# One quarter's attention moved into its own PSUM, the last stores merged over two queues, and the last fifth of a planned kernel in a new order

## The chip, the cores and the metric

The kernel runs on one core of one Trainium2 chip. Its time is device microseconds of one execution. Before the change, three timed runs gave 257.56, 256.4 and 254.25 us; the median, 256.4 us, is the time before. One more execution was profiled; it took 252.56 us.

## The reference

The reference mixes two branches over the same input `x` (2048 rows, 512 channels, bf16) with a gate for each row:

```
g = sigmoid((x * gate_w).sum(-1))
a = long convolution of x with K, plus x * Dskip     # K[d, l] from A, B, C (512 x 128 states), 2048 taps, by FFT
q, k, v = x @ wqkv in 32 heads of 16
phi(z) = [softmax(z @ w_phi), softmax(-(z @ w_phi))]
b = (phi(q) (phi(k)^T v) / (phi(q) . sum phi(k))) @ wo
out = g * a + (1 - g) * b
```

The state-space branch `a` needs, for each channel, a kernel `K` of 2048 taps made from 128 complex exponentials, and then a convolution of 2048 rows with it. The attention branch `b` is linear in the rows once `phi(k)^T v` is known.

## The kernel before, in words

**Layout.** The 2048 rows are held as 16 tiles `j` of 128 rows (row = 64 q + 4 j + c, with q on 32 and c on 4 of the partitions' parts). The 512 channels are four quarters `Q` of 128. `xT` holds the input transposed and later, quarter by quarter, the finished output, from which the stores read.

**Making the taps.** The channels go in 16 units `U` of 32. For one unit (function `kgen`) VectorE builds the table `A` by two products (L1109, L1114) and, unless the unit's digit in `FOURS` is 1, adds them (L1119); it builds `R` by two products (L1126, L1130) from `E` and `cs`, which ScalarE makes. TensorE then multiplies them (L181, tile `kps`): 64 matmuls, or 128 where the sum was left out, since TensorE then adds four terms instead of two. There is one buffer for `A`, so the next unit's L1109 waits for this unit's L181.

**The convolution of a quarter** (function `transform`) runs through TensorE, an eviction to SBUF by ScalarE or VectorE, and so on: `kps`, `KD` (eviction), `psA` (L188), `XA` (eviction), `psB` (L194, or L1228 for the last unit), `XK` (eviction), `t` = `XUX` * `XK` on VectorE (L1302; L1305 and L1240 for units 14 and 15), `psz` (L1328, L1256), `Zr` (eviction). `Zr` goes to DRAM and comes back rearranged as `ZT` (L1343, L1362, on SyncE's queue), or for units 14 and 15 through a transpose on VectorE (`ZS`, L1353 and L1271). Last comes `psy` (L1391) and the multiplication by the gate on VectorE (L1402, L1400), which writes `xT`. Quarters 0 to 2 are done 128 channels at a time, quarter 3 as units 12 and 13 together (64 channels), then 14, then 15, the last one split in halves.

**The attention.** For quarters 0 to 2 the sums of attention are added in the same PSUM tile `psy` by L822 and L824 (`attn`, four matmuls and one for each row tile), before L1391 adds the convolution, so that one multiplication by the gate does both. That holds for row tiles 0 to 11. The attention of tiles 12 to 15 (512 rows) is computed late, in a block of its own (`block(3, True)`): for them the plain convolution of quarters 0 to 2 is copied to `Y` by ScalarE (shown as `Ctab`, whose memory it uses), and a tile `bps` of 512 columns adds up attention of all quarters (L948), the skip term of quarter 3 (L950) and `Y` (L951). It is evicted by L149 (quarter 3) and L983 or L985 (quarters 0 to 2, times the gate) and stored by L997.

**Stores.** Each store of a quarter's output (L1413) is four DMAs, one for each `c`, of 32 partitions. Quarters 0 and 1 are stored as a pair (runs of 512 bytes), quarter 2 alone (256 bytes), quarter 3 in two goes of 64 channels (128 bytes), all by SyncE's queue.

**The order.** Nothing is scheduled when the kernel runs: functions add steps to a plan (`Plan.add`, `Plan.dma`), and `run` walks them in the order of one long string, `ORDER`. That order is at once the order on each engine. Three more strings choose, step by step, between ScalarE and VectorE (`SIDES`), between two rings of PSUM buffers (`RINGS`, two buffers each), and the four-term form (`FOURS`). `NEAR` lists the quarters whose attention of tiles 12 to 15 is added in their own PSUM; it is empty before. Each engine works strictly in its order, so a step that waits holds up all that stand behind it.

Of the kernel before, what the change touches and what calls it, by code (L numbers as in the profile page):

```python
# [10 lines left out]
ACT = mybir.ActivationFunctionType  # L11
# [59 lines left out]
class Plan:  # L71
# [14 lines left out]
             "babhbbclchcCb5b6b7bocDbcdYcibpcHcsd-dZcjctbicIbqbdbebfcmd_9Q9R9SeUcnbwcve0eVbjcue19T9U9Vbkcybxe2brcwe3e4bs9Zczcxcoe59-eL"  # L86
             "cqcp9_cAeMeWcEdOcrdSezeAeBa09W9X9Ya1dTcFbtbubvdRdWcGbycJbze6e7e8cKbAcLblbmbna2cMeRcNcPcQcRcOdQeNe9eaeba3eOc_eSedeeefeceP"
             "d7eQd0d1egd8bBbCbDcScTcUdPeTdUdVeXe-d2d9eYcVcWcXbEbFbGe_dfdgeZdXdhbKdad3dbdncYcZc-bLfAdof0d4d5d6fBbMdcdddef1difVf2djdpfD"
             "bHbIbJf4dqf3ehf5bNfCdrfEf6eibOfWf7ejfeekfGeCeDeEfffFbPfHdkdldmdBbQdsdtduf8eIeJeKdvdwdxf9f_fgfIfafJfhfKdCfXfifYdydzdAfbfc"
             "fdg0fjfkflfZf-eFeGeHfLdEfMdFfNdGdDg1g2dHg3elg4dIdJdKemfmfnfog5g6fpfqfrfOepfPg7eqengadLdMdNeofQg8gbg9fRgderfsbRbSbTgcesbU"  # L90
             "bVbWgffSfTftgeggghgieteuevewexeyfufvfwfxfyfzfUgjgkglgmgngogpgqgr")
    SIDES = ("100001110111000000000101000101010111101001011100000000000100101010000001110001001010100000000000000010000000000000000000"
             "0000000000000001001100000000000000001101100000")
    RINGS = ("101000001110010101100000000000000000000000100000000000000001011100100000001111101101110000100001001110011110100111101101"
             "1010011")
# [716 lines left out]
def plan_queries(P, nc, g, psum, r):  # L812
# [14 lines left out]
    def block(b, late, yn=()):  # L827
        Q, L = Bag(), "L" if late else ""
# [88 lines left out]
        pb, po, ot, out = None, None, [], []  # L917
# [24 lines left out]

        nn = 3 - len(P.NEAR)

# [22 lines left out]
        on = []  # L967
        for ip in range(2 if late else 0):
            j = 4 * b + 2 * ip
# [24 lines left out]
        if late:  # L994
            def st(h):
                for c in (2 * h, 2 * h + 1):
                    (nc.scalar if P.cur.at == "ACT" else nc.sync).dma_start(out=g.out2d[:, 0:128 * nn].rearrange("(q j c) d -> c q j d", q=32, j=16, c=4)[c][:, 4 * b:4 * b + 4],  # L997
                                      in_=xT[32 * c:32 * c + 32, 4 * b:4 * b + 4, 0:nn, :].rearrange("p j a d -> p j (a d)"))
            for h in range(2):
                P.dma("outL", 1.2, 2.0, lambda h=h: st(h), on, move=0.8, cnt=2, eng=("SP", "ACT"))  # L1000
# [67 lines left out]
def plan_conv(P, nc, g, psum, r):  # L1068
# [6 lines left out]
    T, on, yn, late = {}, [], [], []  # L1075
# [130 lines left out]
    def transform(XA, ready, Q, off, nd, Ls, last, co=0, free=True, split=False):  # L1206
# [5 lines left out]
        pair = 1 if Q == 1 and Q not in P.NEAR else 0  # L1212
        lo = 64 if last else off
# [5 lines left out]
        for kk in range(2 if split else 0):  # L1219
# [27 lines left out]
            b = P.add("PE", "psBh", sb, [ready[kk], sk] + ([b] if kk else []), take=[psq, "XK"] + ([] if kk else ["r8"]), drop=(["XA0", "cs"] if kk else []))  # L1247
# [117 lines left out]
        for j0 in range(0, 16, nj):  # L1365
            box = Bag()
            end = j0 + nj == 16
# [42 lines left out]

            def st(h, js=slice(0, 12 if Q < 3 and Q not in P.NEAR else 16)):
                for c in (2 * h, 2 * h + 1):
                    (nc.scalar if P.cur.at == "ACT" else nc.sync).dma_start(out=ov[c][:, js], in_=xT[32 * c:32 * c + 32, js, Q - pair:Q + 1, lo:off + nd].rearrange("p j a d -> p j (a d)"))  # L1413
# [39 lines left out]
    for units in g.LAST:  # L1453
# [5 lines left out]
        end = units[-1] == 15  # L1459
        off = 32 * (units[0] - 12)  # L1460
# [204 lines left out]
```

## Time and profile before

| | before |
|---|---|
| timed runs, median (lowest to highest) | 256.4 us (254.25 to 257.56) |
| the profiled execution | 252.56 us |
| its span, first to last instruction | 250.7 us |
| VectorE, ScalarE, TensorE busy | 93%, 89%, 80% |
| last VectorE operation ends | 244.91 us |
| DMA over the span | 35.65 MB, mean 142 GB/s |

Times inside the execution are microseconds from the start of the span. A row of the timeline is: start, length, engine, line, operation, output<-inputs, shapes, count, and in brackets the idle time ahead of it with what ended it. SPq is SyncE's sequencer, which issues DMAs; the length of such a row is the time for the issue, not for the transfer. An operation's length contains some drain that overlaps the next one, so sums of steps are taken from start to start.

### The profile page before, as it was taken

What the parts mean: (1) busy time and instruction counts of PE and PEld (TensorE: products, weight loads), DVE (VectorE), ACT (ScalarE), POOL (GpSimd) and SP (SyncE); (2) the same over time, 40 slices, a digit from 0 to 9 for tenths busy, and PEclk for the clock granted to TensorE, in tenths of its full rate; (3) what the DMA queues carried; (4) which work ended last, traced back from release to release, by engine and by line L of the source; (5) the groups of instructions that cost most, each with busy time, mean ns of one, the idle gap of its engine ahead of it and who ended that gap; (6) DMA issues with size and microseconds to landing.
All of it is one profiled execution on the core that took longest, in us unless ns stands there. A gap on an engine that the chain in (4) does not pass through costs nothing.

```text
span 250.7 us, 9903 instructions
## 1 busy us (share of the span) xinstructions
PE 201.7 (80%) x4411; PEld 141.6 (56%) x4436; DVE 233.6 (93%) x322; ACT 222.0 (89%) x306; POOL 6.3 (2%) x15
## 2 busy tenths in 40 slices
PE   1478899999965468798878778899999789998970
PEld 1377555456743334255556646775667566877550
DVE  6899999989899997999999999999999999999690
ACT  6799899999999989999999999999999999965340
POOL 5400000000000000000000000000000000000000
PEclk9999999999997759999979999999999999999995
DMA  6799200137290487500528138803797878998775
GB/s 167 162 211 164 77 4 3 42 94 191 53 259 0 126 245 224 169 3 4 151 63 235 30 101 222 277 11 86 189 207 191 222 213 212 239 243 151 184 184 82
DMA packets 62762, 35.65 MB, mean 142 GB/s; under 512 B 42112, under 2 KB 58624, under 8 KB 62336
## 3 DMA queue, kind: packets, MB, share of 16 engines
q1 hardware_dynamic: 62720, 35.03, 57.1%
q8 instruction: 34, 0.56, 1.0%
q14 instruction: 8, 0.07, 0.1%
HBM read 21.91 MB, written 13.11 MB: 140 GB/s over the span
## 4 chain that ended last, share of the span: by engine, by line
DVE 40%; PE 19%; ACT 16%; SPq 8%; issue 8%; DMA 7%; DVEq 0%; ACTq 0%
DVE R L1126 5%; DVE t L1302 4%; DVE A L1109 4%; DMA XUX<-XUd 3%; ACT Eq L68 3%; PE vp L755 3%; SPq L1531 3%; DVE A L1114 3%; PE pk L707 3%; DVE R L1130 3%; DVE Zk L734 2%; SPq L214 2%; DVE E L1061 2%; PE psB L614 2%; DVE Eq L912 2%
## 5 line engine op out<-in xcount | busy, mean ns | idle before, releaser
L181 PEld LDWEIGHTS <-A 128*32 128x32 bf16 x1664 | 28.4, 160 | 6.3 <-issue 3.4
L181 PE MATMUL kps<-R,A 128*32 128x64 bf16 x1664 | 30.2, 230 | 1.9 <-DVE A L1114 0.6
L68 ACT ACTIVATE cs<-args 128x1024 bf16<-128x1024 f32 x32 | 30.8, 1049 | 0.4 <-PE args L1025 0.4
L1130 DVE TENSOR_TENSOR R<-E,cs 128x2048 bf16<-128x2048 bf16 x16 | 19.5, 1220 | 0.0
L1109 DVE TENSOR_TENSOR A<-Ctab,Dtab 128x2048 bf16<-128x2048 bf16 x16 | 19.5, 1220 | 0.0
L1126 DVE TENSOR_TENSOR R<-E,cs 128x2048 bf16<-128x2048 bf16 x16 | 19.5, 1220 | 0.0
L1114 DVE TENSOR_TENSOR A<-Ctab,Dtab 128x2048 bf16<-128x2048 bf16 x16 | 19.5, 1220 | 0.0
L147 ACT CAST Zr<-psz 128x1024 bf16<-128x1024 f32 (+1 forms) x17 | 16.5, 975 | 2.7 <-issue 1.2
L147 ACT CAST XK<-psB 128x1024 bf16<-128x1024 f32 (+1 forms) x15 | 15.1, 1012 | 3.9 <-PE psB L194 2.3
L147 ACT CAST XA<-psA 128x1024 bf16<-128x1024 f32 (+1 forms) x16 | 15.6, 1008 | 3.2 <-PE psA L188 3.2
L755 PE MATMUL vp<-WW,xT 128*128 128x512 bf16 x59 | 17.5, 414 | 0.8 <-issue 0.7
L614 PE MATMUL psB<-XAu,TB 64*128 64x128 bf16 x256 | 11.8, 248 | 7.4 <-ACT xst L147 5.2
L1302 DVE TENSOR_TENSOR t<-XUX,XK 128x2048 bf16<-128x2048 bf16 x14 | 17.1, 1220 | 0.3 <-ACT XK L147 0.3
L68 ACT ACTIVATE Ek<-pk 128x512 bf16<-128x512 f32 x32 | 16.8, 603 | 0.4 <-PE pk L707 0.2
L68 ACT ACTIVATE Eq<-pq 128x512 bf16<-128x512 f32 (+1 forms) x28 | 16.8, 715 | 0.2 <-PE pq L841 0.2
L68 ACT ACTIVATE E<-args 128x1024 bf16<-128x1024 f32 x16 | 16.8, 1060 | 0.0
L1328 PE MATMUL psz<-t,TI 128*128 128x512 bf16 x49 | 14.6, 380 | 2.0 <-ACT cs L68 0.5
L841 PE MATMUL pq<-xT,Wqp 128*128 128x512 bf16 x64 | 15.7, 381 | 0.6 <-ACT Eq L68 0.6
L614 PEld LDWEIGHTS <-TB 64*128 64x128 bf16 x256 | 9.5, 109 | 11.3 <-issue 11.1
L707 PE MATMUL pk<-WW,xT 128*128 128x512 bf16 x57 | 15.5, 380 | 0.5 <-issue 0.2
L734 DVE TENSOR_REDUCE Zk<-Ek 128x64 f32<-128x1024 bf16 x12 | 14.0, 1211 | 0.0
L65 ACT ACT_TABLE_LOAD x10 | 12.8, 1283 | 0.2
(215 smaller groups left out, 492.4 us busy)
## 6 DMA issues: line engine op xcount, KB each, us to landing
XUX<-XUd SPq DMA_DIRECT2D x24, 256.0 KB, 4.1
XUd<-xst SPq DMA_DIRECT2D x8, 512.0 KB, 3.1
ax<-apd SPq DMA_DIRECT2D x16, 256.0 KB, 4.7
Zd<-Zr SPq DMA_DIRECT2D x14, 256.0 KB, 4.0
ZT<-Zd SPq DMA_DIRECT2D x12, 256.0 KB, 5.3
UD<-in_A_u_dram SPq DMA_DIRECT2D x16, 128.0 KB, 4.2
XUd<-xst SPq DMA_DIRECT2D x8, 256.0 KB, 4.0
XUX<-XUd SPq DMA_DIRECT2D x4, 512.0 KB, 6.3
```

The source lines that it names most:

```text
L68: return self.nc.scalar.activation(**kw)
L147: self.nc.scalar.copy(out=o, in_=i)
L181: nc.tensor.matmul(kps[32 * dj:32 * dj + 32, g4, e, :], lhsT=A[:, ka, :, :, d].rearrange("p a b -> p (a b)"), rhs=R[:, kr, d, :], start=(i ...
L614: nc.tensor.matmul(box.ps[:, c2, sl, :], lhsT=fc.TB[rows, b0:b0 + 2].rearrange("p a b -> p (a b)"), rhs=X.t[rows, k, r0 + sl].rearrange("p ...
L707: nc.tensor.matmul(box.ps[:], lhsT=xT[:, st, kt, :], rhs=g.WW[:, kt, :], start=(kt == 0), stop=(kt == 3))
L734: nc.vector.tensor_reduce(out=K.Z[:, u].rearrange("p g h -> p (g h)"), in_=K.E[:, u].rearrange("p g (h f) -> p (g h) f", f=16), axis=mybir ...
L755: nc.tensor.matmul(box.ps[:], lhsT=xT[:, st, kt, :], rhs=g.WW[:, 4 + kt, :], start=(kt == 0), stop=(kt == 3))
L1109: nc.vector.tensor_tensor(out=c.A[:, 0:2].rearrange("p o a b c -> p (o a) b c"), in0=g.C[U // 8][:, 0:2, :, d0 % 256:d0 % 256 + 32].rearra ...
L1114: nc.vector.tensor_tensor(out=c.A[:, 2:4].rearrange("p o a b c -> p (o a) b c"), in0=g.C[U // 8][:, 1:3, :, d0 % 256:d0 % 256 + 32].rearra ...
L1126: nc.vector.tensor_tensor(out=c.R[:, :, :, 32:64], in0=t.E[:, 1].unsqueeze(1).to_broadcast([128, 2, 32, 32]), in1=t.cs[:], op=ALU.mult)
L1130: nc.vector.tensor_tensor(out=c.R[:, :, :, 0:32], in0=t.E[:, 0].unsqueeze(1).to_broadcast([128, 2, 32, 32]), in1=t.cs[:, ::-1, :, ::-1], o ...
L1302: nc.vector.tensor_tensor(out=box.t, in0=Ls[r0 // ns].X[:], in1=box.XK[:].unsqueeze(1).to_broadcast([128, 2, 1024]), op=ALU.mult)
```

## The change

1. `NEAR` becomes `(2,)`: quarter 2 (channels 256 to 383) takes the attention of row tiles 12 to 15 in its own `psy` tile, like the other twelve. The late block is therefore planned ahead of quarter 2's convolution; the `Y` copy of quarter 2 is gone, its second multiplication by the gate covers eight row tiles instead of four (L1402 for L1400), and `bps` holds quarters 0, 1 and 3: L948 is now two matmuls (256 and 128 columns) where one had 512, L951 has 256 columns, L983 and L985 256 columns, and the stores of L997 runs of 512 bytes instead of 768. Quarter 2's store has all 16 row tiles.
2. Quarter 3 is stored once, at the end, in runs of 256 bytes: two of its four DMAs by SyncE's queue, two by ScalarE's, which issued no DMA before. The store of 64 channels ahead of it is gone.
3. Unit 13 takes the four-term form (`FOURS`): its L1119 is gone, its L181 has 128 matmuls instead of 64.
4. The last fifth of `ORDER`, `SIDES` and `RINGS` are new. Ahead of it all engines keep their rows.

```diff
-             "babhbbclchcCb5b6b7bocDbcdYcibpcHcsd-dZcjctbicIbqbdbebfcmd_9Q9R9SeUcnbwcve0eVbjcue19T9U9Vbkcybxe2brcwe3e4bs9Zczcxcoe59-eL"
+             "babhbbclchcCb5b6b7bocDbccPcibpcHcscRcQcjctbicIbqbdbebfcmcS9Q9R9SeTcnbwcvcTeUbjcucU9T9U9VbkcybxcVbrcwcWcXbs9ZczcxcocY9-eK"
...
-    FOURS = ("0111111101011000")
+    FOURS = ("0111111101011100")
     BOTHE = ("0000000000000000")
-    NEAR = ()
+    NEAR = (2,)
...
             def st(h):
                 for c in (2 * h, 2 * h + 1):
-                    (nc.scalar if P.cur.at == "ACT" else nc.sync).dma_start(out=g.out2d[:, 0:128 * nn].rearrange("(q j c) d -> c q j d", q=32, j=16, c=4)[c][:, 4 * b:4 * b + 4],
+                    nc.sync.dma_start(out=g.out2d[:, 0:128 * nn].rearrange("(q j c) d -> c q j d", q=32, j=16, c=4)[c][:, 4 * b:4 * b + 4],
                                       in_=xT[32 * c:32 * c + 32, 4 * b:4 * b + 4, 0:nn, :].rearrange("p j a d -> p j (a d)"))
             for h in range(2):
-                P.dma("outL", 1.2, 2.0, lambda h=h: st(h), on, move=0.8, cnt=2, eng=("SP", "ACT"))
+                P.dma("outL", 1.2, 2.0, lambda h=h: st(h), on, move=0.8, cnt=2)
...
-        lo = 64 if last else off
+        lo = 0 if last else off
...
-            if end and (Q != 0 or 1 in P.NEAR) and (nd > 32 or last):
+            if end and (Q != 0 or 1 in P.NEAR) and (Q < 3 or last):
                 for h in range(2):
-                    P.dma("out", 1.2, 2.0, lambda h=h, st=st: st(h), on, move=(1.6 if pair else 1.05 if nd == 128 else 0.9), cnt=2, eng=("SP", "ACT") if Q == 3 else "SP")
+                    P.dma("out", 1.2, 2.0, lambda h=h, st=st: st(h), on, move=(1.6 if pair else 1.4 if Q == 3 else 1.05), cnt=2, eng="ACT" if Q == 3 and h else "SP")
                 on.clear()
```

The order of VectorE where the two kernels part, at about 201 us of the profile before. L1302 is quarter 2's `t`, L912 the late block's second product, L1109 to L1130 units 13 and 14, L1402 quarter 1's gate. Before:

```order
L1302 TENSOR_TENSOR t<-XUX,XK 128x2048
L912 TENSOR_TENSOR Eq<-Eq,ax 128x2048
L1109 TENSOR_TENSOR A<-Ctab_75,Dtab 128x2048
L1126 TENSOR_TENSOR R<-E,cs 128x64x32
L1302 TENSOR_TENSOR t<-XUX,XK 128x2048
L1114 TENSOR_TENSOR A<-Ctab_75,Dtab 128x2048
L1130 TENSOR_TENSOR R<-E,cs 128x64x32
L1119 TENSOR_TENSOR A<-A 128x2048
L1302 TENSOR_TENSOR t<-XUX,XK 128x2048
L1402 TENSOR_TENSOR xT<-psy,gT 128x8x128
```

Now:

```order
L912 TENSOR_TENSOR Eq<-Eq,ax 128x2048
L1302 TENSOR_TENSOR t<-XUX,XK 128x2048
L1109 TENSOR_TENSOR A<-Ctab_75,Dtab 128x2048
L1302 TENSOR_TENSOR t<-XUX,XK 128x2048
L1114 TENSOR_TENSOR A<-Ctab_75,Dtab 128x2048
L1126 TENSOR_TENSOR R<-E,cs 128x64x32
L1130 TENSOR_TENSOR R<-E,cs 128x64x32
L1402 TENSOR_TENSOR xT<-psy,gT 128x8x128
L1302 TENSOR_TENSOR t<-XUX,XK 128x2048 x2
L1109 TENSOR_TENSOR A<-Ctab_75,Dtab 128x2048
L1126 TENSOR_TENSOR R<-E,cs 128x64x32
L149 CAST XA<-psA 128x32x32
L1114 TENSOR_TENSOR A<-Ctab_75,Dtab 128x2048
```

The late block's product moved ahead of `t`, unit 13's sum (L1119) is gone, and an eviction of `XA` that ScalarE did stands a little later on VectorE.

The end of VectorE's order. `KD`, `KDb`, `XAb`, `XK` and L1240 belong to unit 15, L1305 and L1353 to unit 14, the rows with `bps` to the late block. Before:

```order
L149 CAST KD<-kps 128x256
L149 CAST KDb<-kps 128x256
L149 CAST xT<-bps 128x2x128
L149 CAST XAb<-psA 128x512
L1305 TENSOR_TENSOR t<-XUX,XK 128x2x512 x2
L149 CAST XK<-psB 128x512
L1240 TENSOR_TENSOR t<-XUX,XK 128x2x512
L985 TENSOR_SCALAR xT<-bps,gT 128x384
L1353 STREAM_TRANSPOSE ZS<-Zr 128x1024
L1402 TENSOR_TENSOR xT<-psy,gT 128x16x64
L1271 STREAM_TRANSPOSE ZS<-Zr 128x1024
```

Now:

```order
L1305 TENSOR_TENSOR t<-XUX,XK 128x2x512
L1402 TENSOR_TENSOR xT<-psy,gT 128x8x128
L149 CAST XAb<-psA 128x512
L149 CAST xT<-bps 128x2x128
L985 TENSOR_SCALAR xT<-bps,gT 128x256
L1240 TENSOR_TENSOR t<-XUX,XK 128x2x512 x2
L1353 STREAM_TRANSPOSE ZS<-Zr 128x1024
L1271 STREAM_TRANSPOSE ZS<-Zr 128x1024
L1402 TENSOR_TENSOR xT<-psy,gT 128x16x64
```

`KD`, `KDb` and unit 15's `XK` left VectorE for ScalarE, the two L1240 stand together, and the gate of the 64 channels moved behind both transposes.

The end of SyncE's order, the stores; two DMAs of the same shape as the last row's stand last on ScalarE.

```order
-L1413 DMA out_dram<-xT 32x12x128 x2
+L1413 DMA out_dram<-xT 32x12x256 x2
 L1362 DMA ZT<-Zd_0_122 32x2048 x4
-L1413 DMA out_dram<-xT 32x12x128 x2
-L1413 DMA out_dram<-xT 32x12x256 x4
-L997 DMA out_dram<-xT 32x4x384 x4
-L1413 DMA out_dram<-xT 512x1x64 x8
+L1413 DMA out_dram<-xT 512x1x128 x4
+L997 DMA out_dram<-xT 32x4x256 x4
+L1413 DMA out_dram<-xT 32x12x256 x2
+L1413 DMA out_dram<-xT 512x1x128 x2
```

Half of the pair's store moved ahead of `ZT`, the other half behind the late block's store, and eight DMAs of 64 channels became two here and two on ScalarE.

More of the change, by code (lines that the diff above doesn't have):

```diff
@@ L94 @@
-    RINGS = ("101000001110010101100000000000000000000000100000000000000001011100100000001111101101110000100001001110011110100111101101"
-             "1010011")
+             "000000000111000000000100000000000010000")
+    RINGS = ("101000001110010101100000000000000000000000100000000000000001011100000000001111101100010111100110100100011010110100010001"
+             "1011001")
     WARM = ("000000000000000000000000000000000000000000000000000000000000000000000000000000000000000000000000000000000000000000000000"
```

11 lines of the change are left out of this document (5 added, 6 removed).

## The prediction

> **What bounds the kernel now.** I read the page first, for the engine that carries the span.
>
> ```profile
> span 250.7 us, 9903 instructions
> PE 201.7 (80%) x4411; PEld 141.6 (56%) x4436; DVE 233.6 (93%) x322; ACT 222.0 (89%) x306; POOL 6.3 (2%) x15
> DVE 40%; PE 19%; ACT 16%; SPq 8%; issue 8%; DMA 7%; DVEq 0%; ACTq 0%
> ```
>
> VectorE carries it, but a share over the span hides stages, so the second view is busy time by stretch, over the part that the change touches.
>
> ```profile
> 205.00:215.00 10.00, 9.48 (x200) 6.95 (x200) 10.00 (x10) 9.86 (x11) 0.00 (x0) 1.00 0.96 230
> 215.00:225.00 10.00, 9.81 (x215) 8.27 (x215) 10.00 (x11) 8.37 (x10) 0.00 (x0) 1.00 1.02 246
> 225.00:229.00 4.00, 3.43 (x100) 3.01 (x99) 3.97 (x4) 1.93 (x2) 0.00 (x0) 1.00 0.82 122
> 229.00:234.00 5.00, 4.67 (x129) 3.35 (x129) 3.24 (x6) 1.60 (x2) 0.00 (x0) 1.00 0.93 193
> 239.00:245.00 6.00, 4.38 (x202) 3.02 (x200) 5.34 (x7) 1.70 (x4) 0.00 (x0) 1.00 0.77 175
> 245.00:250.70 5.70, 0.00 (x0) 0.00 (x0) 0.00 (x0) 0.00 (x0) 0.00 (x0) 0.52 0.52 80
> ```
>
> The columns are TensorE, its weight loads, VectorE, ScalarE, GpSimd, the granted clock, the DMA share and GB/s. There are three stages. Up to 229 us VectorE never rests and TensorE rests 0.52 + 0.19 + 0.57 = 1.3 us in 24. From 229 to 245 nobody is full: unit 15 goes alone through a chain of short steps. From 245 on only stores run. The third view is the timeline, for the last two stages.
>
> ```profile
> 228.17 1.23 DVE L1119 TENSOR_TENSOR A<-A 128x2048 bf16<-128x2048 bf16 x1
> 229.92 0.69 DVE L1400 TENSOR_TENSOR xT<-psy,gT 128x512 bf16<-128x512 f32 x1 [0.52 <-PE psy L1391]
> 231.66 0.41 DVE L149 CAST KD<-kps 128x256 bf16<-128x256 f32 x1
> 234.83 0.69 DVE L149 CAST XAb<-psA 128x512 bf16<-128x512 f32 x1 [0.76 <-ACT XA L147]
> 237.69 0.69 DVE L1240 TENSOR_TENSOR t<-XUX,XK 128x1024 bf16<-128x1024 bf16 x1
> 238.82 0.68 DVE L1240 TENSOR_TENSOR t<-XUX,XK 128x1024 bf16<-128x1024 bf16 x1
> 240.59 1.18 DVE L1402 TENSOR_TENSOR xT<-psy,gT 128x1024 bf16<-128x1024 f32 x1
> 241.69 1.22 DVE L1271 STREAM_TRANSPOSE ZS<-Zr 128x1024 bf16<-128x1024 bf16 x1
> 244.49 0.42 DVE L1402 TENSOR_TENSOR xT<-psy,gT 128x256 bf16<-128x256 f32 x1 [0.39 <-PE psy L1391]
> ```
>
> VectorE's last operation ends at 244.91, and the span 5.78 us later. I split the change at three points: the start of unit 15's `kps`, the start of its `psB` (L1228), and that end. The work is reckoned against the profiled execution, 252.56 us, which is 1.9 us over its span and 1.5% below the median of the runs, 256.4.
>
> **The change part by part.** *Up to unit 15's `kps`.* The rows on TensorE:
>
> ```profile
> 201.25 2.25 PE L181 MATMUL kps<-R,A 128*32 128x64 bf16 x128 [0.29 <-ACT XK L147]
> 210.53 1.22 PE L181 MATMUL kps<-R,A 128*32 128x64 bf16 x64
> 227.40 0.39 PE L1377 MATMUL psy<-diagD,xT 128*128 128x128 bf16 x4
> 227.62 0.81 PE L194 MATMUL psB<-XA,TB 128*128 128x32 bf16 x26
> 229.80 1.22 PE L181 MATMUL kps<-R,A 128*32 128x64 bf16 x64
> 231.28 1.02 PE L948 MATMUL bps<-wo,oT 128*128 128x512 bf16 x3 [0.27 <-ACT Ctab L147]
> 233.53 0.41 PE L188 MATMUL psA<-W,KD 128*64 128x128 bf16 x8
> 234.10 1.04 PE L948 MATMUL bps<-wo,oT 128*128 128x512 bf16 x4
> 236.28 0.55 PE L1228 MATMUL psB<-XA,TB 128*128 128x32 bf16 x16
> 236.68 0.55 PE L1228 MATMUL psB<-XAb,TB 128*128 128x32 bf16 x16
> ```
>
> VectorE first:
>
> ```profile
> 201.24 1.23 DVE L1302 TENSOR_TENSOR t<-XUX,XK 128x2048 bf16<-128x2048 bf16 x1 [0.29 <-ACT XK L147]
> 202.38 1.22 DVE L912 TENSOR_TENSOR Eq<-Eq,ax 128x2048 bf16<-128x2048 bf16 x1
> 203.54 1.23 DVE L1109 TENSOR_TENSOR A<-Ctab,Dtab 128x2048 bf16<-128x2048 bf16 x1
> L149 DVE CAST XAu<-psA 128x1024 bf16<-128x1024 f32 x7 | 8.4, 1217 | 0.2 <-PE psA L589 0.2
> ```
>
> From 201 us to unit 15's last table operation there are 26 operations before and after: unit 13's sum (L1119, 1.23 us, a step of 1.14 as from 201.24 to 202.38) goes, and one `XA` eviction of 1024 columns comes, at 1217 ns for the nearest kind: even. L912 standing first fills the 0.29 us wait, from about 200.9. But unit 13's L1109 is then reached two steps later, at 203.2, and needs the one `A` buffer, which unit 12's `kps` gives back 2.25 us after its start; with the late block's L931 now ahead of it on TensorE I take 201.5 for that, so 203.8. What was gained is lost again in a wait of 0.65, and unit 15's tables are complete at 229.6 instead of 229.40.
>
> TensorE gets 64 more matmuls for unit 13 (2.25 - 1.22 = 1.0 us) and the attention of four more row tiles: five matmuls of 128 columns each, 2560 columns. Two row tiles of `bps` have 5120 columns (each 4x512 + 128 + 384) and take 2.25 us (231.28 to 233.53), so 1.1; L1377's 512 columns go (0.22, from 227.40 to 227.62). Together 1.9 us, between 201 and 229.8. The cover is TensorE's idle time there: 1.3 us from the windows and the 0.29 at 201. Unit 15's `kps` starts at 230.1 if all of it is covered, at 231.7 if none. One thing holds TensorE besides:
>
> ```profile
> 215.57 1.03 ACT L147 CAST Zr<-psz 128x1024 bf16<-128x1024 f32 x1
> 220.25 1.71 SPq L1362 DMA_DIRECT2D ZT<-Zd  x4
> ```
>
> Quarter 2's last `Zr` ends at 216.6, and 3.65 us on SyncE fetches it as `ZT`, for the `psy` ahead of unit 15's `kps`. In the new order this `Zr` stands behind two `E` and an `oT` on ScalarE, by my count 1.1 us later, and `ZT` with it: some 0.7 us of TensorE, in part time that it would have rested anyway. Walking the rows in the new order with these steps I get 230.2, 0.4 later than before, and take it: it is the covered end, since unit 13's matmuls fall into a stretch in which TensorE waits for VectorE's tables.
>
> *From there to `psB`.* Before, `KD` waited for VectorE, which was in two gate operations (229.92 to 231.66), and `psA` for two row tiles of `bps` (231.28 to 233.53). Now ScalarE evicts both halves. A cast of 256 columns by ScalarE has no row; the nearest is
>
> ```profile
> L68 ACT ACTIVATE apm<-zs 128x256 bf16<-128x256 f32 x4 | 1.7, 418 | 0.3 <-DVE zs L884 0.3
> ```
>
> so two end 0.8 us after `kps`, covered by `bps`. Two row tiles of `bps` now have 2 x (4x(256 + 128) + 128 + 256) = 3840 columns, in proportion 1.65 us for 2.25, if a matmul of 128 columns costs its columns alone, as L1377's four do. From the end of `kps` (start plus 1.14) to `psA` it took 2.6 us and takes 1.65; from `psA` to `psB` 2.75 and now 2.2. `psB` starts at 230.2 + 1.14 + 1.65 + 2.2 = 235.2: 1.1 us earlier.
>
> *From `psB` to VectorE's end.* Before, the first L1240 came 1.4 us after `psB`, the second 1.13 us later with a L985 between, and the last transpose 2.9 us after that, 1.1 of it behind the gate of the 64 channels (240.59). Now the second L1240 follows the first by its own 0.6, and the transposes come ahead of that gate: 235.2 + 1.4 + 0.6 + 1.8 = 239.0, and 239.2 since the other transpose stands in between. Then VectorE has 1.2 us for it, that gate (1.1), 512 columns (0.6) and twice 256 (0.4 each), to 242.8, with TensorE's products inside. This stretch shrinks from 8.6 to 7.6. VectorE ends at 242.8 instead of 244.9: **2.1 us earlier**. ScalarE's added casts lie in its rests (1.60 of 5 us busy), and `Y` of quarter 2, with the 0.27 us that `bps` waited for it, is gone.
>
> *The stores.*
>
> ```profile
> 245.73 2.60 SPq L1413 DMA_DIRECT2D out_dram<-xT  x4
> out_dram<-xT SPq DMA_DIRECT2D x8, 64.0 KB, 2.2
> 245.80:249.50 3.70, 0.00 (x0) 0.00 (x0) 0.00 (x0) 0.00 (x0) 0.00 (x0) 0.50 0.65 102
> 236.60:237.80 1.20, 1.15 (x29) 0.77 (x26) 1.17 (x4) 0.49 (x1) 0.00 (x0) 1.00 0.91 157
> 239.66 2.69 SPq L997 DMA_DIRECT2D out_dram<-xT  x4
> ```
>
> Before, SyncE was 0.8 us late for the last four (still issuing the first four of 64 channels), issued one each 0.65 us, so the last at 247.7, and landed it 2.2 us later, 0.8 before the end. The engines were only 65% busy: the issue set the pace. Now two queues issue two each, in 1.3 us, but 512 KB hang on VectorE's end instead of 256. Runs of 256 bytes moved at 157 GB/s at a share of 0.91, so 173 at full: 3.0 us. Beside that stand 0.1 to the issue, the 2.2 of landing less a transfer of 64 KB at 102 GB/s (0.64), so 1.55, and 0.8 to the end: 5.5 us after VectorE, **0.3 less** than 5.78. The bounds: if the two queues' issue set the pace, 0.1 + 0.65 + 2.2 + 0.8 = 3.75, a gain of 2.0; if ScalarE's queue, of which no row shows an issue, moves its half only at the old 102 GB/s, 5.1 us of transfer, a loss of 1.8. I take 5.5 by the row with runs of the same size. SyncE is free in time: L997 took 2.69 us with larger runs, and its stores and the pair's two end ahead of 242.8 if they start by 238.
>
> The Trainium skill, "DMA: Bandwidth & Descriptors", section "Rules for kernel authors", says that spreading DMAs over SyncE and ScalarE brings no bandwidth, as all run on the same 16 engines, and saves issue time alone, and that small transfers are best merged; its fit in "Anatomy of one DMA" (for GpSimd's path) is 2.0 us plus the bytes at 436 GB/s. By that fit 512 KB would take 3.2 us, and the estimate for the tail would be 4.1, a gain of 1.7; the row of 157 GB/s speaks against its rate here.
>
> The sum: 2.1 + 0.3 = 2.4 us; the execution 252.56 - 2.4 = 250.2, in proportion to the median 253.9.
>
> **The rivals.** *The engines eat the order's gain.* TensorE's 1.9 us aren't covered, `kps` starts at 231.7 and VectorE ends at 244.3. For it: 98% busy from 215 to 225. Against it: the rests elsewhere. With the tail's 0.3 the gain is 0.9, and the time 255.5 us.
>
> *The tail follows the issue.* The engines keep up with two queues, since nothing else uses SBUF then. 2.1 + 2.0, and 0.4 more if `kps` isn't late: 4.1 to 4.5 us, 251.8 to 252.2. Against it: 173 GB/s. This is also the side to which the Trainium skill's fit in "DMA: Bandwidth & Descriptors" leans.
>
> *The single `A` buffer makes it slower.* L1109 of the next unit waits for `kps` of the last, and unit 13's `kps` now lasts twice as long. `A` can come late to units 13, 14 and 15 in turn. I reckoned 0.65 at the first and no wait at the others, where the walk leaves 0.8 us of slack or less; a `kps` held up by a PSUM buffer that ScalarE frees late, in any of the three, passes straight to VectorE. It turns to slower when these waits exceed 0.65 + 2.4 = 3.1 us; at 4.5 us the execution takes 254.0, or 257.8 by the median. For it: VectorE at 10.00 of 10.00 has no rest to make up in. Against it: three late places are needed.
>
> *The change doesn't do what it says* where the late block isn't ready for quarter 2: but its evictions stand ten rows and more ahead of that use on ScalarE, so this gets no share.
>
> **How the numbers follow.** Forecast 0.54; eaten 0.20; issue-paced 0.14; slower 0.12. The likeliest gives 253.9. Three runs of before spread from -0.8% to +0.5% of their median, so a case is some 1.5 us wide on each side. The range from 251.0 to 257.0 takes in the middle of the issue-paced case with its scatter and most of the slower one. Two per cent is 5.1 us, about what a measurement of this kernel can tell from no change: under 251.3 lies only the lower part of the issue-paced case, 0.10 with the scatter; over 261.5 almost nothing, 0.04; within, 0.86.
>
> **What would show it.** Unit 15's `kps` at 230 to 231, its L1228 about a microsecond ahead of 236.28, VectorE's last L1402 ending near 242.8, and the span 5.5 us behind it with a DMA share near 1 for three microseconds. A wait of some 0.65 us ahead of unit 13's L1109. The forecast is wrong if L1109 waits more than a microsecond at two places, if `kps` of unit 15 starts behind 232, or if the tail is under 4 or over 7 us.

## The result, and the profile after

The changed kernel took 257.38 us (median of 6 runs, 255.06 to 259.76) against 254.92 us of the kernel before on the same chip (251.61 to 257.56): 1.0123 times as long, with a 95% interval of 1.0076 to 1.0170. A second set gave 1.0108 (1.0047 to 1.0170). The forecast was 253.9 us, 2.4 us less than before; by the two ratios the change costs 3.1 and 2.7 us.

The profile shown below is of the second set: 255.89 us, span 254.1. (The first set's profiled execution was a disturbed one, 259.76 us with a span of 258.0; it has the same waits at the same places, some of them longer.) The head of the page, with the chain's shares:

```profile
span 254.1 us, 10118 instructions
PE 204.8 (81%) x4532; PEld 143.7 (57%) x4532; DVE 232.4 (91%) x319; ACT 221.3 (87%) x307; POOL 5.6 (2%) x15
PE 28%; DVE 27%; ACT 18%; DMA 10%; SPq 7%; issue 7%; DVEq 0%; ACTq 0%
```

VectorE's share of the chain fell from 40% to 27%, TensorE's rose from 19% to 28%. The stretches of the changed part (columns as in the prediction):

```profile
205.00:215.00 10.00, 10.00 (x240) 7.61 (x240) 10.00 (x9) 9.53 (x10) 0.00 (x0) 1.00 0.95 232
215.00:225.00 10.00, 9.12 (x231) 7.44 (x229) 9.01 (x11) 7.24 (x9) 0.00 (x0) 1.00 0.86 224
225.00:232.00 7.00, 6.68 (x161) 4.95 (x160) 7.00 (x7) 4.44 (x5) 0.00 (x0) 1.00 0.95 204
232.00:238.00 6.00, 5.08 (x140) 4.40 (x127) 3.55 (x5) 2.24 (x6) 0.00 (x0) 1.00 0.90 184
246.20:254.10 7.90, 0.00 (x0) 0.00 (x0) 0.00 (x0) 0.00 (x0) 0.00 (x0) 0.64 0.55 92
```

TensorE is now full, 10.00 of 10, where it had rests before, and what it lacks in the next two rows is 0.88 and 0.32. The last row is the tail: 7.9 us with no engine at work and the DMA engines 55% busy. TensorE's timeline around the two places where it stood still, and quarter 2's first `psB`, from which the stages below are counted (a row's bracket is the idle time ahead; "issue" means that no semaphore explains it):

```profile
200.55 1.10 PE L194 MATMUL psB<-XA,TB 128*128 128x128 bf16 x16 [1.43 <-ACT XA L147]
216.99 0.25 PE L188 MATMUL psA<-W,KD 128*64 128x128 bf16 x2 [0.88 <-issue]
232.27 0.38 PE L181 MATMUL kps<-R,A 128*32 128x64 bf16 x10
233.56 1.05 PE L181 MATMUL kps<-R,A 128*32 128x64 bf16 x54 [0.92 <-issue]
238.52 0.56 PE L1228 MATMUL psB<-XA,TB 128*128 128x32 bf16 x16
```

Unit 15's `kps` is broken behind its tenth matmul. VectorE, with its last operation in the last row:

```profile
217.28 1.23 DVE L149 CAST XA<-psA 128x1024 bf16<-128x1024 f32 x1 [0.86 <-PE psA L188]
230.52 1.23 DVE L1130 TENSOR_TENSOR R<-E,cs 128x2048 bf16<-128x2048 bf16 x1
237.66 0.69 DVE L149 CAST XAb<-psA 128x512 bf16<-128x512 f32 x1 [2.45 <-ACT XA L147]
239.73 1.29 DVE L1240 TENSOR_TENSOR t<-XUX,XK 128x1024 bf16<-128x1024 bf16 x2 [0.19 <-ACT XK L147]
243.73 2.44 DVE L1402 TENSOR_TENSOR xT<-psy,gT 128x1024 bf16<-128x1024 f32 x4
```

And the queues at the end: SyncE's last rows, ScalarE's only one, and, from the view of waits, SyncE's entry for these stores (total, times, longest):

```profile
241.82 1.79 SPq L997 DMA_DIRECT2D out_dram<-xT  x4
243.66 6.96 SPq L1413 DMA_DIRECT2D out_dram<-xT  x4
246.25 1.37 ACTq L1413 DMA_DIRECT2D out_dram<-xT  x2
SPq L1413 <- DMA out_dram<-xT: 4.8, 1, 4.8
```

Four stores take SyncE 6.96 us, and 4.8 of it is one wait for another store's landing.

The stages of both kernels, worked out from start to start in each profile: from quarter 2's first `psB` (L194, the sixteen matmuls near 200 us, behind which the orders part) to unit 15's `kps`, from there to its L1228 (stage two), to VectorE's end, to the span's end (the tail). (The start of this count differs by a microsecond between executions, in rows that both kernels share.)

```
                 psB->kps  kps->L1228  L1228->VectorE's end  ->span's end
before             30.25      6.48            8.63               5.78
before, again      29.95      6.36            8.64               5.29
changed, first     32.67      8.20            7.64               7.95
changed, again     31.72      6.25            7.65               7.93
predicted          30.65      4.99            7.6                5.5
```

Against the mean of the two profiles of before, the changed kernel's second profile is +1.62, -0.17, -0.99 and +2.39: +2.85 us in all, as the runs say. The forecast was +0.4, -1.5, -1.0 and -0.3. So the third stage came as foretold, and the 5.2 us of error lie in the tail (2.7), in `kps` to `psB` (1.3) and ahead of `kps` (1.2).

### The profile page after: what moved, and what is told of

Read it like the earlier page. It is cut to its first block, busy times and chain, and to the rows that moved or that the text cites. A ratio compares the mean times of both kernels' runs of the same rounds, so it can differ in the third digit from the quotient of the medians.

```text
span 258.0 us, 10118 instructions
## 1 busy us (share of the span) xinstructions
PE 205.2 (80%) x4532; PEld 143.5 (56%) x4532; DVE 233.1 (90%) x319; ACT 221.3 (86%) x307; POOL 6.2 (2%) x15
## 4 chain that ended last, share of the span: by engine, by line
DVE 31%; ACT 22%; PE 21%; DMA 8%; SPq 8%; issue 7%; DVEq 0%; ACTq 0%
ACT cs L68 5%; ACT Eq L68 4%; PE kps L181 4%; SPq L1531 4%; ACT E L68 3%; PE pk L707 3%; DVE vr L764 2%; DVE t L1302 2%; DVE Zk L734 2%; SPq L214 2%; ACT L65 2%; ACT XA L147 2%; PE psy L822 2%; PE vp L755 2%; DMA UD<-in_A_u_dram 2%
## 5 line engine op out<-in xcount | busy, mean ns | idle before, releaser
L181 PE MATMUL kps<-R,A 128*32 128x64 bf16 x1728 | 31.9, 230 | 5.0 <-issue 3.6
L181 PEld LDWEIGHTS <-A 128*32 128x32 bf16 x1728 | 29.7, 161 | 9.3 <-issue 6.1
L1109 DVE TENSOR_TENSOR A<-Ctab,Dtab 128x2048 bf16<-128x2048 bf16 x16 | 19.5, 1217 | 1.9 <-PE kps L181 1.9
L1130 DVE TENSOR_TENSOR R<-E,cs 128x2048 bf16<-128x2048 bf16 x16 | 19.5, 1216 | 0.0
L1302 DVE TENSOR_TENSOR t<-XUX,XK 128x2048 bf16<-128x2048 bf16 x14 | 16.9, 1216 | 0.5 <-ACT XK L147 0.5
L841 PE MATMUL pq<-xT,Wqp 128*128 128x512 bf16 x64 | 16.4, 395 | 0.6 <-ACT Eq L68 0.6
L1328 PE MATMUL psz<-t,TI 128*128 128x512 bf16 x60 | 15.2, 380 | 1.3 <-DVE t L1302 0.5
L147 ACT CAST KD<-kps 128x1024 bf16<-128x1024 f32 (+2 forms) x9 | 8.2, 906 | 8.4 <-PE kps L181 8.4
L147 ACT CAST XA<-psA 128x1024 bf16<-128x1024 f32 (+1 forms) x15 | 14.7, 1002 | 0.2 <-PE psA L188 0.2
```

Of the source, the lines that this page charges most:

```text
L147: self.nc.scalar.copy(out=o, in_=i)
L181: nc.tensor.matmul(kps[32 * dj:32 * dj + 32, g4, e, :], lhsT=A[:, ka, :, :, d].rearrange("p a b -> p (a b)"), rhs=R[:, kr, d, :], start=(i ...
L1109: nc.vector.tensor_tensor(out=c.A[:, 0:2].rearrange("p o a b c -> p (o a) b c"), in0=g.C[U // 8][:, 0:2, :, d0 % 256:d0 % 256 + 32].rearra ...
L1130: nc.vector.tensor_tensor(out=c.R[:, :, :, 0:32], in0=t.E[:, 0].unsqueeze(1).to_broadcast([128, 2, 32, 32]), in1=t.cs[:, ::-1, :, ::-1], o ...
L1302: nc.vector.tensor_tensor(out=box.t, in0=Ls[r0 // ns].X[:], in1=box.XK[:].unsqueeze(1).to_broadcast([128, 2, 1024]), op=ALU.mult)
```

## The experiments

Two theories were formed from the two traces. *Late stores*: stores of SyncE wait for stores of ScalarE, through semaphores that both queues count up. *Pieces*: TensorE's rows are fetched in pieces, and it stands still where one comes late. Both have the rivals that the expectations state.

### The same two kernels once more

No edit.

> The changed kernel once more. Theory of the late stores (SyncE's second pair store and its last store stand behind the landing of ScalarE's stores): the second pair store is again issued only after ScalarE's first store has landed, and the span ends 7.5 to 8.5 us behind VectorE's end. Theory of TensorE's stalls as a part of the program: waits of over 1 us that no semaphore explains come back at the same places (in units 13 to 15's L181), and unit 15's kps starts again behind 233. Rival, that those stalls were an accident of the one profiled execution: they are gone or elsewhere, kps starts at 230 to 232, and VectorE ends near 245.

> The kernel before once more, as a measure of what one execution differs from the next. If stalls of TensorE without a semaphore (0.58 us in all behind 100 us in the first profile) are as common in it as in the changed kernel (5.1 us), one sees several of over 0.4 us here too, and the span is 252 to 255 us; if they belong to the changed kernel, no more than one, and 250 to 252 us. The time ratio to itself shows the scatter: 0.995 to 1.005.

The ratio of before to itself was 0.9992 (0.9952 to 1.0033), its span 249.7 us. In the changed kernel the late stores came back (tail 7.93) and so did two of the five stalls of its first profile, at the same instructions: L188 near 217 and unit 15's `kps` behind ten matmuls. The stalls near 191, 196 and 207 were gone or under 0.2 us, and `kps` started at 232.27, not behind 233. In before there was none of over 0.25 us behind 200. So some stalls belong to the changed program; how long each is differs from one execution to the next.

### All last stores by SyncE

```diff
-                    P.dma("out", ..., cnt=2, eng="ACT" if Q == 3 and h else "SP")
+                    P.dma("out", ..., cnt=2, eng="SP")
```

> All four last stores by SyncE, the rest as changed. Theory of the late stores: nothing on SyncE waits for ScalarE any more; the pair's second store goes out right behind its first, the last four are issued 0.65 us apart from VectorE's end on, the last at +2.05, landing 2.2 to 3 us later: the span ends 5.0 to 6.0 us behind VectorE's end instead of 8.0, and the time is 2 to 3 us under the changed kernel's. Rival, that 512 KB in runs of 256 bytes take that long whichever queue issues them: 7 us or more behind VectorE's end, and the time within 1 us of the changed kernel's.

The time fell to 1.0011 (0.9977 to 1.0045) of before, 2.5 us under the changed kernel by the two ratios. VectorE's last row and SyncE's last two of this run:

```profile
244.49 2.45 DVE L1402 TENSOR_TENSOR xT<-psy,gT 128x1024 bf16<-128x1024 f32 x4
242.57 2.15 SPq L997 DMA_DIRECT2D out_dram<-xT  x4
244.77 4.82 SPq L1413 DMA_DIRECT2D out_dram<-xT  x6
```

Six stores now take 4.82 us where four took 6.96, and the span (252.8) ends 5.86 us behind VectorE. The whole cause can be read in the order of the changed program, with what each store waits for. The pair's second store and SyncE's last two:

```
L1413 DMA out_dram<-xT 32x12x256 [waits DMAHW1_49]
L1413 DMA out_dram<-xT 512x1x128 [waits DMAHW2_49,DVE_49]
L1413 DMA out_dram<-xT 512x1x128 [waits DMAHW3_49]
```

and the two of ScalarE:

```
L1413 DMA out_dram<-xT 512x1x128 [waits DMAHW1_49,DVE_49,Activation_49]
L1413 DMA out_dram<-xT 512x1x128 [waits DMAHW3_49]
```

Each DMA counts up one of eight semaphores at its landing, in turn, and waits for the landing of the one that had it before. ScalarE's two stores got their turn on `DMAHW1` and `DMAHW3` ahead of SyncE's pair store and last store. So the pair's second store, whose data was long there, waited for a store of ScalarE that itself waits for VectorE's end, and SyncE's half of the last store stood behind it. In the changed kernel's second profile ScalarE's first store was issued at 246.25 and landed at 248.92; SyncE's held-up stores went out at 248.94, 249.35 and 249.98.

### Two queues without that wait

SyncE's stores in another order (only `ORDER` changes): the pair whole, then half of the late block's, quarter 2's, the other half. By it no SyncE store shares a turn with ScalarE's. The rows of all other engines keep their order. The difference on SyncE:

```
-L1413 DMA out_dram<-xT 32x12x256 x2
+L1413 DMA out_dram<-xT 32x12x256 x4
 L1362 DMA ZT<-Zd_0_122 32x2048 x4
+L997 DMA out_dram<-xT 32x4x256 x2
 L1413 DMA out_dram<-xT 512x1x128 x4
-L997 DMA out_dram<-xT 32x4x256 x4
-L1413 DMA out_dram<-xT 32x12x256 x2
+L997 DMA out_dram<-xT 32x4x256 x2
 L1413 DMA out_dram<-xT 512x1x128 x2
```

> Two queues as changed, but SyncE's stores in another order (pair, half of the late block's, quarter 2, other half of the late block's), by which none of them waits on a semaphore that ScalarE's stores count up. Theory of the late stores: both queues issue two each right at VectorE's end, the span ends 3.8 to 5.5 us behind it, and the time is 2.5 to 4 us under the changed kernel's. Rival, that ScalarE's queue itself is slow (issue or transfer): 7 us or more, with ScalarE's stores landing last, though nothing waits. If the transfer at 173 GB/s bounds it: 5.5 us; if the issue does: 3.8 to 4.7.

Time 1.0067 (1.0033 to 1.0101) of before, tail 6.41 us, not the 3.8 to 5.5 expected. The last rows of both queues; VectorE ended at 247.88:

```profile
247.75 1.10 SPq L997 DMA_DIRECT2D out_dram<-xT  x2
248.96 1.56 SPq L1413 DMA_DIRECT2D out_dram<-xT  x2
247.96 1.38 ACTq L1413 DMA_DIRECT2D out_dram<-xT  x2
```

ScalarE's two went out at once and were issued in 1.38 us, and they landed at 251.08 and 252.10, ahead of SyncE's last at 253.20. So ScalarE's queue isn't what holds the end, and the 4.8 us wait is gone. But this order keeps SyncE at older stores for a microsecond after VectorE's end, and the tail is no shorter than with one queue. A gain of two queues over one was not shown; an order in which SyncE is also free at VectorE's end was not run.

### Where TensorE's rows are cut into pieces

The page's list of queues (packets, MB, share) has one for instructions:

```profile
q8 instruction: 35, 0.57, 1.0%
```

These are 35 transfers of 16 KB, and the changed kernel's trace holds 9,088 rows of TensorE (matmuls, weight loads and the rest): 256 rows to a transfer. Counting the rows in the trace's records gives a place to every unexplained rest of TensorE behind 185 us that is over 0.25 us, here for three profiles:

```
run               row number (mod 256)   at (us)  idle (us)  line
changed, first    6337 (193)             190.97   0.47       L181 kps, unit 10
changed, first    6593 (193)             196.34   1.29       L181 kps, unit 11
changed, first    7105 (193)             206.99   1.04       L1025
changed, first    7617 (193)             218.68   0.52       L188 psA
changed, first    8385 (193)             236.36   1.81       L181 kps, unit 15
changed, again    7617 (193)             216.99   0.88       L188 psA
changed, again    8385 (193)             233.56   0.92       L181 kps, unit 15
last_sp           6337 (193)             192.14   1.09       L181 kps, unit 10
last_sp           7617 (193)             218.00   0.61       L188 psA
last_sp           8385 (193)             234.31   1.02       L181 kps, unit 15
```

All lie at the border of a piece. In every one, TensorE went on 1.2 to 1.7 us after the end of a transfer and 2.2 to 2.9 us after its start. The Trainium skill, "Runtime: NRT & Kernel Launch", section "Instruction fetch mechanics", says that instructions are refilled in blocks of 16 KiB, 256 each, and that crossing a border is mostly hidden. The size agrees, and so does "mostly": of some 35 borders in each of these profiles five, two and three show such a rest. Those few cost 0.5 to 1.8 us each, and in the changed kernel's second profile both of them, 0.88 and 0.92 us, lie on the chain that ended last.

The test shifts the borders and leaves the other work as it is: matmuls of 32 columns, into a PSUM tile whose real matmuls overwrite them, at quarter 2's first `psB`, ahead of which TensorE rests. The number is 32 in the run on before, and 20 and 68 in two on the changed kernel.

```diff
                 box.ps = psum([128, ns, nd], "psB")
+                for _ in range(32 if Q == 2 and r0 == 0 else 0):
+                    nc.tensor.matmul(box.ps[0:32, 0, 0:32], lhsT=g.ident[:, 0:32], rhs=g.ident[:, 0:32], start=True, stop=True, ...)
```

> The kernel before with 32 such matmuls at the same place, and nothing else changed. Theory of the pieces: borders move 64 rows ahead, and one comes into unit 15's kps (near 230.3) behind a piece of 2.8 us: TensorE stalls there for 1.2 to 1.6 us, as it does in the changed kernel, and psB of unit 15 and all behind it come that much later: the time 1 to 1.8 us over the kernel before. Rival: the kernel before has no such stall because its order is another; no stall in kps, and the time within 0.4 us of the kernel before.

This is the clearest of the runs: the kernel before, with 32 such matmuls, takes 1.0109 (1.0071 to 1.0147) of its time, 2.8 us more. Its TensorE:

```profile
199.20 0.95 PE L1286 MATMUL psB<-ident 128*32 128x32 bf16 x32 [1.44 <-ACT XA L147]
200.09 1.07 PE L194 MATMUL psB<-XA,TB 128*128 128x128 bf16 x16
229.46 0.22 PE L822 MATMUL psy<-wo,oT 128*128 128x128 bf16 x1 [1.12 <-issue]
231.23 1.16 PE L181 MATMUL kps<-R,A 128*32 128x64 bf16 x58
233.74 0.31 PE L181 MATMUL kps<-R,A 128*32 128x64 bf16 x6 [1.35 <-issue]
233.97 1.89 PE L948 MATMUL bps<-wo,oT 128*128 128x512 bf16 x4
```

The first two rows show that the added matmuls do not use the rest. They wait for the same `XA` as the real ones, start behind the rest and put `psB` off by 0.89 us; 20 of them put it off by 0.58 and 68 by 1.78. So the times of these four runs contain up to that much of the added work itself. The places and lengths of the stalls, and the stages that are counted from `psB` on, do not.

The stall in `kps` is where it was expected, with another ahead of it, and the cost is greater than the stalls: `bps` takes 1.89 us for four matmuls that took 1.02. The granted clock of the stretch (eighth number), in this run and then in the kernel before without them:

```profile
235.00:240.00 5.00, 5.00 (x36) 2.31 (x34) 1.24 (x3) 1.43 (x3) 0.00 (x0) 0.76 0.74 181
```

```profile
235.00:240.00 5.00, 4.67 (x113) 2.59 (x111) 4.96 (x9) 2.79 (x5) 0.00 (x0) 1.00 0.89 187
```

Two shorter stretches of this run, up to the stall's end and behind it:

```profile
230.53:233.94 3.41, 2.06 (x105) 1.80 (x101) 1.82 (x2) 1.60 (x2) 0.00 (x0) 1.00 0.71 180
233.94:237.35 3.41, 3.41 (x14) 1.29 (x10) 0.76 (x2) 0.00 (x0) 0.00 (x0) 0.50 0.65 139
```

Behind the stall the clock was 0.50 for 3.41 us, and stage two took 9.41 us instead of 6.36. The changed kernel's first profile has the same (granted clock 0.66 from 235 to 240, stage two 8.20); its second kept 1.00 (6.25). The Trainium skill, "TensorE: Matmul & The Clock Gate", section "What's actually happening", gives half the rate after an idle window of about 3.4 us. The half agrees; but the 3.41 us ahead of it were not idle here, TensorE was busy for 2.06 of them. A stall alone doesn't decide it: behind the 0.92 us in `kps` of the changed kernel's second profile the clock stayed at 1.00.

> The changed kernel with 20 matmuls of 32 columns that nobody reads, ahead of quarter 2's first psB (near 200 us), where TensorE rests for 1.4 us. Theory of the pieces: TensorE's rows come in pieces of 16 KB, 256 rows each, and a piece that TensorE gets through in under some 4.2 us makes it wait for the next; so a stall belongs to a place in the program. The 40 added rows move every later border 40 rows ahead. Unit 15's kps is no longer broken behind its tenth matmul, nor psA (L188) near 217; borders fall instead into kps of unit 12 (near 204, a stall of under 1 us) and L931 near 214 (about 1 us, behind which little waits). From kps to psB of unit 15 5.2 to 5.5 us instead of 6.25 or 8.2; the time 1 to 2 us under the changed kernel's. Rival, that the stalls come from the order of work or from the DMA traffic at that time: kps is broken as before, and the time is the same within 0.5 us, or 0.4 longer for the added matmuls.

> The same with 68 such matmuls, 1.2 us of TensorE in a rest of 1.4. Theory of the pieces: a border now falls into the psy of unit 15's last halves (L1385, near 244.6), behind a piece of 256 rows that takes some 2.3 us, and one into L181 of unit 13 near 212 (3.3 us); unit 15's kps is whole. TensorE stalls for 1.5 to 2 us right ahead of VectorE's last operations, and the time is about the changed kernel's, at most 0.5 under it and up to 1.5 over. Rival, that stalls belong to the work or the traffic: kps is broken as before, no stall near 244, and the time as the changed kernel's.

Twenty matmuls in the changed kernel made `kps` whole, as expected:

```profile
215.95 0.38 PE L931 MATMUL ops<-Eq,KVbd 128*128 128x256 bf16 x2 [1.41 <-issue]
232.86 1.23 PE L181 MATMUL kps<-R,A 128*32 128x64 bf16 x64
238.01 0.55 PE L1228 MATMUL psB<-XA,TB 128*128 128x32 bf16 x16
```

Stage two took 5.15 us, near the 5.0 predicted. But the time stayed at 1.0109 (1.0048 to 1.0171): the other border, now at L931 with 1.41 us, was not harmless. `psA` stands behind it, and VectorE waited 1.35 us for that at 217.80. The twenty matmuls' own 0.58 us is in that time too. With 68 one stall ahead of the added matmuls came back (1.32 at 197.55); behind them the stalls lay in L181 near 216.7 (0.38), in `bps` at 238.09 (0.57) and in the last `psy` at 248.72 (0.99), `kps` was whole, and the time 1.0120 (1.0077 to 1.0164). The places were right; that less than 1.5 us came at the last `psy` was not.

> Last stores by SyncE alone and 20 matmuls ahead of psB: both repairs at once. If they add up (1.9 us for the stores, 1 to 2 us for the border), the time is 3 to 4 us under the changed kernel's, 0.5 to 2 us under the kernel before: what is left of the forecast's gain of 2.4 us. If only the stores count, it is last_sp's time, equal to the kernel before within 0.5 us.

That is the edit of last_sp and 20 matmuls. Both together took 1.0026 (0.9989 to 1.0063), not the 0.5 to 2 us under before that adding up would give. Its profile has stage two at 5.13 us, a stall of 2.26 us at L931 and one of 0.57 in the `psy` ahead of `kps`.

### Looking for borders that cost nothing

The same matmuls, at other places: 78 and 38 of them in two `psB` of the first part (they start at 77.52 and 87.67 us), with the last stores by SyncE; and the same matmuls in before.

```diff
                 box.ps = psum([128, 2, 4, 128], "psB")
+                for _ in range({0: 78, 16: 38}.get(r0, 0) if h == 1 else 0):
+                    nc.tensor.matmul(box.ps[0:32, 0, 0, 0:32], lhsT=g.ident[:, 0:32], rhs=g.ident[:, 0:32], start=True, stop=True, ...)
```

> Last stores by SyncE alone, and 116 matmuls of 32 columns that nobody reads, in TensorE's rests near 78 and 85 us (78 and 38 of them, some 2.1 us). All later borders of the pieces move 232 rows ahead, that is 24 rows back; by the row times of the changed kernel's second profile, no piece behind 207 us is then run through in less than 4.2 us, where the 20 matmuls had put one of 3.2 us at L931, which cost as much as it saved. Theory of the pieces: no stall over 0.3 us behind 207, VectorE without a wait for psA near 217, unit 15's kps whole and 1 to 2 us earlier against quarter 2's first psB (200.55 to 232.27 in the second profile, 31.7 us; now 30.3 to 31), psB 5.2 to 5.5 us behind kps; the time 1.5 to 3 us under last_sp's, so 1 to 2.5 us under the kernel before. Rival, that stalls only move about, or the new order is no better without them: the kernel before's time within 0.5 us.

> The kernel before with the same 116 matmuls. By its row times no piece behind 195 us is run through in less than 4.2 us then, as is so now but for one near 205; so the theory of the pieces expects the kernel before's time within 0.6 us. If the added matmuls themselves speed something up (a higher granted clock from 80 to 100 us) or slow it down, it shows here, and this is the kernel against which the order of the changed one is to be judged.

The first took 0.9990 (0.9952 to 1.0028) of before, not the 1 to 2.5 us less that were expected; the second took 1.0027 (0.9991 to 1.0064). The two intervals overlap: with the same added matmuls, too, the new order with one queue was not shown to beat the old one. Both profiles have stalls where the kernels without the matmuls show none over 0.25 us in their second profiles: 1.82 and 1.72 us near 140, and 0.92 and 0.90 near 197. In the first, L188 was free of its stall, but `kps` was broken again, twelve matmuls later, by 1.16 us:

```profile
234.29 0.56 PE L181 MATMUL kps<-R,A 128*32 128x64 bf16 x22
236.01 0.87 PE L181 MATMUL kps<-R,A 128*32 128x64 bf16 x42 [1.16 <-issue]
```

TensorE had needed 4.19 us for the piece ahead of this stall, which is right at the limit of 4.2 that should be safe. Other pieces refute the limit: in the changed kernel's second profile the one ahead of L188 took 4.55 us and stalled, and one near 191 took 3.50 and did not. What starts a transfer isn't the passing of the border before; in these profiles it started anywhere from 2 to 254 rows behind it.

Next, the same with one entry of `ORDER` moved, the late block's first L931 behind unit 12's `kps`:

```diff
-...eOd8dLePeSepd9...
+...eOdLePeSd8epd9...
```

> As sp_pad116, and on TensorE the late block's first L931 behind unit 12's kps instead of ahead of it. Theory of the single A buffer: kps of unit 12 starts 0.9 us earlier and VectorE's wait ahead of unit 13's L1109 (0.0 to 1.2 us in the profiles so far) is gone; unit 15's tables come 0.3 to 0.8 us earlier, the time up to 0.8 us under sp_pad116's. If that wait has slack behind it, or if the late block then comes late to VectorE, the time is the same within 0.3 us or longer.

The wait for `A` ahead of unit 13's table (L1111 in this kernel) fell from 1.18 to 0.71 us, and the time rose to 1.0114 (1.0067 to 1.0160). VectorE and, below it, ScalarE and TensorE:

```profile
212.02 1.22 DVE L1128 TENSOR_TENSOR R<-E,cs 128x2048 bf16<-128x2048 bf16 x1 [3.02 <-ACT cs L68]
```

```profile
207.30 1.01 ACT L147 CAST oT<-ops 128x1024 bf16<-128x1024 f32 x1 [3.22 <-PE ops L933]
```

```profile
205.39 1.87 PE L933 MATMUL ops<-Eq,KVbd 128*128 128x256 bf16 x8
```

ScalarE's `oT` waits 3.2 us for the late block's product that was moved back, `cs` stands behind it, and VectorE waits 3.0 us for `cs`. Some 0.8 us of that is not the order: the granted clock was 0.50 from 203.69 to 207.10, and the product took 1.87 us where it took 1.04 in the run with 116 matmuls. Nor did `kps` of unit 12 come 0.9 us earlier, but 0.2, counted from `psB`, since it then waited for an eviction. The move made a longer wait than the one it shortened; what the single `A` buffer alone costs here, this run doesn't show.

Last, 70 and 36 matmuls at the first two places and 42 more at the head of quarter 2's first `psy`:

```diff
+                for _ in range({0: 70, 16: 36}.get(r0, 0) if h == 1 else 0):
...
             def pya(j0=j0, box=box):
                 box.ps = psum([128, 2, 512], "psy")
+                for _ in range(42 if Q == 2 and j0 == 0 else 0):
+                    nc.tensor.matmul(box.ps[0:32, 0, 0:32], lhsT=g.ident[:, 0:32], rhs=g.ident[:, 0:32], start=True, stop=True, ...)
```

> Last stores by SyncE alone, and two groups of added matmuls of 32 columns: 70 and 36 in the rests near 78 and 85 us, and 42 at the head of quarter 2's first psy, in front of the rest in which L1391 waits for ZT (0.5 to 0.7 us near 228). By the profiles so far a border is reached without a stall where its piece was fetched 2.9 us or more ahead of it. With these numbers the border near 217 moves 44 rows back, out of psA (L188) into the part behind psz, and unit 15's moves 40 rows ahead, out of kps into the psy in front of it. Theory of the pieces: no stall near 217, VectorE without a wait for psA there, kps of unit 15 whole, at most 0.8 us of stall in L1391 ahead of it; from row tile 12's first attention matmul of quarter 2's predecessors (L822 near 185.5 us) to VectorE's end 59.0 to 60.0 us, where the changed kernel's second profile has 60.4 and the two of the kernel before 60.6 and 59.8; time 0.5 to 1.5 us under the kernel before. If the new order is worth nothing even without stalls: 60.5 or more, and the kernel before's time or above it.

The time was 1.0054 (1.0010 to 1.0098) of before, and no gain. Behind 210 us there was no stall at all, `kps` was whole and stage two took 5.15 us; but a border at 209.8 now cost 1.75 us, one near 197 cost 1.62 with a granted clock of 0.50 in the 3.41 us behind it, and the 42 matmuls took 1.34 us, where a rest of 0.87 us had stood in the run with 116. Moving the borders moved the stalls; a changed kernel with none was not made.

## Why the prediction was wrong

**The stores** failed, by 2.7 us, and it is the largest step. "Now two queues issue two each, in 1.3 us" left out what a store waits for besides its data, and so did "its stores and the pair's two end ahead of 242.8": the pair's second store was held to 248.94. A wait was added, and the question of who is queued behind it on SyncE was not put. The wait stood in the program's order before any run. None of the rivals held it; two of the signs given for being wrong did: the tail of over 7 us, and `kps` behind 232 (232.27 and 234.17). The estimate of 5.5 us was nearer to what one queue needs (5.86 to 6.31 in the runs of this order with it). The bound of 3.75 and the rival *the tail follows the issue* were not reached in any run. No run shows a gain from merging the stores either: the order before, with eight smaller ones, needed 5.29 to 6.84 us in the four profiles that have it.

**From `kps` to `psB`** the step was right and its cover was not. In the three runs in which `kps` was whole without a lowered clock or another stall behind it, the stage took 5.13 to 5.15 us for the 4.99 predicted; in the changed kernel it took 6.25 and 8.20. The term that failed is "start plus 1.14" for `kps` itself: a border of a piece broke it, by 0.92 to 1.81 us. The trace of before showed no such stall there, only one of 0.58 us at 229.01, ahead of `kps`. (Two sums of this part are off, by too little to matter: 3840 to 5120 of 2.25 us is 1.69, not 1.65, and the steps up to VectorE's end add up to 242.9.)

**Up to unit 15's `kps`** +0.4 was predicted and +1.6 measured (the second profile), with a stall of 0.88 at L188, of which VectorE's 0.86 at 217.28 is the consequence. Without the stalls of their own stretch the changed order's profiles come to +0.5 to +1.3 (31.35 - 0.77 in last_sp, 31.86 - 0.49 in clean_two_b, against 30.10); that is subtraction, not a run. The rival *the engines eat the order's gain* is thereby probably part of the answer: from 205 to 215 us TensorE had its rests filled (10.00 of 10), so that the cover of 1.3 us that the step named was used up. That each stall went through to `kps` for this reason is argued, not tested. The wait of 0.65 at unit 13's L1109 was well placed in the middle of what came (0.1 to 1.3 over the runs of this order).

**The single `A` buffer** forecast the right side and nearly the right time (257.8) by a wrong way, and that is luck: its waits at units 13 to 15 came to 1.3 us or less in every run but the last, where they were 1.27 and 0.66; it needed 3.1.

**From `psB` to VectorE's end** was right: 7.64 to 7.66 in the changed kernel and six of its variants (8.13 and 8.48 in the other two: TensorE waited 0.54 us for `ZT` in one, and a stall of 0.99 lay in the other), 7.6 predicted, 8.6 before.

So the order does give back 1.0 us there and 1.3 behind an unbroken `kps`. The crossed semaphores take 2.1 (7.93 to 5.86), the border in `kps` some 1.1 (6.25 against 5.15), and up to `kps` the stall at L188 and the order itself share 1.6 in a way that is worked out by subtraction alone. What stays open: what starts the transfer of a piece, what lowers the clock behind some stalls and not behind others, and whether the new order with one queue would beat before if TensorE did not stall. With one queue the two are equal, at 1.0011 and 0.9990.

## What to carry to other kernels

When a store or load moves to another queue, read in the built order what each DMA of both queues waits for: a completion semaphore taken in turn can make a transfer that is ready wait for one that is issued last of all. Where an engine runs thousands of short instructions, adding or removing a hundred anywhere moves the fetch borders behind it, so an edit should be judged with its stalls told apart by profile, and a difference of 1% may be largely that. A rest that covers an added cost covers it once: what else used it comes out behind. And work that waits for what ended the rest stands behind the rest, not in it, as the added matmuls did.

## What was not expected of the hardware

A fetch of 256 rows for TensorE cost up to 2.26 us at one border; where TensorE stood still at a border behind 185 us, it went on 2.2 to 2.9 us after the transfer's start. 32 matmuls that nobody reads, of 0.9 us, made an unchanged kernel 1.1% slower (1.0109), with two new stalls of 1.12 and 1.35 us in its profile. The second was followed by a granted clock of 0.50 for 3.41 us, which by subtraction cost more than the stall did: stage two grew by 3.05.
